# A new first list for a one-core attention and mixture kernel: loads of the seventh pair of token tiles placed earlier, GpSimd products for the sign words of eight weight chunks, TensorE low parts for the first eight chunks

## The chip, the cores and the metric

One core of one Trainium2 chip runs the kernel. The metric is device microseconds of one execution, as the median of several runs. In the profile PE is TensorE, DVE is VectorE, ACT is ScalarE, POOL is GpSimd and SP is SyncE, whose queue issues most of the transfers.

## The reference

Three stages follow one another. The first is attention inside chunks of 64 positions, the second a channel mixing layer, the third four experts of causal attention with a choice of two. The change lies in the part that does the first two. Batch is 8, sequence 576, eight heads of 64, 512 channels, 1024 hidden channels.

```python
scores = scale * np.matmul(q_c, k_c.transpose(0, 1, 2, 4, 3))   # 64 x 64 blocks
attn = softmax(scores)                                           # with max and 1e-9
out = np.matmul(attn, v_c)
...
xk = mu_k * x + (1.0 - mu_k) * x_prev
xr = mu_r * x + (1.0 - mu_r) * x_prev
k = np.maximum(xk @ w_k, 0.0)
v = k * k @ w_v
r = 1.0 / (1.0 + np.exp(-(xr @ w_r)))
x2 = r * v
...
out = _moe2_ref(x=x2, w_gate, wq, wk, wv, wo)
```

The weights w_r, w_k and w_v come as 64-bit floats. Each product of the mixing layer is formed from a high and a low fp32r part of both operands, three matmuls in place of one.

## The kernel before

The 4608 tokens are cut in 36 tiles of 128 for the attention and in 12 units of 384 for the mixing. Two tiles make a pair j. A pair's steps are, in the letters of the order lists: lq, lk, lv (loads through SP's queue, two buffers for each of q, k, v), Tq and Tk (transposes: by PE for tiles 0 to 11, by DVE for tiles 12 and later, since `by_dve` holds from the seventh pair on), Eq and Ek (ACT's copies out of PSUM), S (scores on PE), X, U, E, Z, Y (maximum, subtraction, exponential, sum, scaling), Tp and Ep (transposed probabilities), V (products with v on PE) and W (ACT's copies into the unit's tile XT). A unit's steps are prev (the column before a segment), a, b, c, d with r or k (ACT's scaled previous column, DVE's multiply-add, ACT's high part, DVE's low part of the mixed input, four channel groups each), r, k and v (12 matmuls each on PE; a k or an r needs all four d of its unit; v comes in two halves), s, K, J, y, z, x, D behind them.

The 20 weight chunks (128 x 512 numbers of 64 bits, 512 KB each) are turned into high and low parts on the way: chunks 0 to 3 belong to w_r, 4 to 11 to w_k, 12 to 19 to w_v. L loads a chunk, A (ACT) scales the upper words, G (DVE, two instructions, lines 430 and 431) puts sign and last bits together, B (DVE, line 435) joins, H (POOL, line 84) casts the high part, O (DVE, line 446) subtracts to get the low part. There are two buffers for the joined chunk (`cz`); O is the last to read one.

The order is written out. `follow(START)` emits the steps of the first list one by one, and `in_line` binds each instruction behind the one before it on its own engine, so that every engine and SP's queue run in the list's order, whatever waits. START covers the attention of tiles 0 to 11, units 0 and 1 and the beginning of unit 2, and all chunks; `TWO_UNITS` follows four times. Its first steps are Tq1 and Tq0, which there mean tiles 13 and 12. A step that waits holds up all behind it on its engine: a load that waits for a buffer holds up all later loads.

Of the kernel before, what the change touches and what calls it, by code (L numbers as in the profile page):

```python
# [20 lines left out]
START = """
L7 A7 G7 B7 L3 G3 L5 H7 O7 A3 B3 H3 lk0 L6 lq0 Tq0 L1 A5 G5 B5 L14 H5 lk1 Tk0 O3 A6 G6 B6 lq1 Eq0 L2 Tk1 H6 O5 G1 O6
A1 B1 A14 Ek1 G14 H1 O1 lk2 B14 H14 Ek0 G2 O14 Tq1 Eq1 S0 mu A2 B2 X0 H2 O2 lk3 L4 A4 Tk2 Ek2 U0 E0 G4 Z0 lq2 Tq2 lq3
Eq2 Tk3 lv1 B4 Y0 Tq3 L11 G11 H4 Ek3 Eq3 S1 X1 A11 B11 H11 Tp1 Ep1 U1 lv0 Tp0 O11 Ep0 lq5 Tq5 lq4 V0 O4 E1 Z1 Y1 W0 L0
Tq4 A0 lk5 G0 lk4 Tk5 L8 G8 Ek5 B0 Eq5 Eq4 H0 Tk4 Ek4 Tp3 Ep3 Tp2 Ep2 S2 X2 lv2 O0 lv3 L19 A8 V1 W1 prev0 U2 A19 G19
ar0,2 br0,2 ar0,0 br0,0 E2 Z2 cr0,2 dr0,2 lq7 Tq7 lk6 Tk6 Eq7 cr0,0 dr0,0 Y2 lq6 Tq6 Eq6 lk7 Tk7 Ek6 ar0,1 br0,1 ar0,3
Ek7 br0,3 cr0,1 lq8 Tq8 Tp4 B8 Ep4 lk8 S3 cr0,3 H8 Eq8 dr0,1 ak0,2 Tk8 Ek8 Tp5 lq9 Tq9 dr0,3 r0,0 r0,1 X3 bk0,2 lv5
ak0,1 Ep5 bk0,1 Eq9 U3 O8 ck0,2 ck0,1 lk9 Tk9 B19 H19 lv4 V2 dk0,1 dk0,2 E3 Z3 lq11 Tq11 s0,1 r0,2 r0,3 Ek9 S4 ak0,0
bk0,0 ak0,3 bk0,3 W2 prev1 ck0,3 ck0,0 L10 s0,3 G10 dk0,3 A10 s0,2 lk10 s0,0 dk0,0 k0,0 k0,1 k0,2 O19 L9 G9 B10 H10
ar1,0 lv7 br1,0 A9 B9 lk11 Tk11 lq10 Tq10 H9 Eq11 O10 L17 Y3 K0,0 O9 K0,1 J0,1 L18 cr1,0 dr1,0 A17 ar1,1 lk13 K0,2 G17  # L30
J0,0 ar1,2 A18 k0,3 Tp6 Ep6 br1,1 G18 k0,4 J0,2 lv6 k0,5 B18 H18 Tp7 cr1,1 K0,4 dr1,1 B17 O18 H17 J0,4 ar1,3 K0,3
br1,2 cr1,2 br1,3 k0,6 k0,7 cr1,3 K0,6 L13 A13 L12 O17 J0,3 K0,7 dr1,2 dr1,3 r1,0 r1,1 G13 A12 Ep7 B13 H13 Eq10 s1,0
L15 G12 B12 Ek11 V3 O13 J0,7 G15 s1,1 H12 O12 A15 W3 B15 L16 r1,2 Tk10 r1,3 A16 G16 Ek10 S5 s1,2 H15 O15 K0,5 B16 H16
lv9 ak1,1 J0,6 J0,5 s1,3 v0,0,0 O16 v0,0,1 ak1,3 bk1,3 X4 v0,1,0 v0,1,1 ck1,3 v0,2,0 v0,2,1 bk1,1 ck1,1 dk1,1 U4 ak1,0
E4 bk1,0 y0,1 z0,1 x0,1 D0,1 y0,0 dk1,3 ak1,2 bk1,2 ck1,0 dk1,0 v0,3,0 ck1,2 dk1,2 v0,3,1 k1,0 K1,0 z0,0 x0,0 y0,2
z0,2 D0,0 k1,1 K1,1 Z4 Y4 Tp9 Tp8 Ep8 y0,3 lv8 X5 J1,1 U5 k1,2 k1,3 x0,2 Ep9 K1,2 k1,4 k1,5 J1,2 D0,2 J1,0 K1,3 J1,3
K1,4 z0,3 x0,3 k1,6 k1,7 E5 J1,4 K1,5 K1,6 J1,5 K1,7 v1,0,0 J1,6 V4 W4 J1,7 v1,0,1 prev2 v1,1,0 ak2,1 D0,3 lv11 v1,1,1
v1,2,0 v1,2,1 Z5 Y5 Tp10 bk2,1 y1,0 ar2,2 br2,2 v1,3,0 cr2,2 v1,3,1 z1,0 y1,1 x1,0 D1,0 dr2,2 ar2,0 br2,0 ck2,1 dk2,1
cr2,0 dr2,0 ar2,3 br2,3 ar2,1 br2,1 Ep10 cr2,3 z1,1 x1,1 D1,1 Tp11 dr2,3 y1,2 z1,2 cr2,1 dr2,1 r2,0 r2,1 x1,2 ak2,3
bk2,3 ck2,3 dk2,3 s2,0 ak2,2 y1,3 ak2,0 s2,1 r2,2 r2,3 z1,3 lv10 Ep11 V5 s2,2 x1,3 D1,3 bk2,0 ck2,0 s2,3 bk2,2 ck2,2  # L40
lv13 lk12 D1,2 W5 lq13 lv12 lq12 dk2,0 dk2,2
""".split()
# [1001 lines left out]
```

## Time and profile before

| what | us |
|---|---|
| median of 3 runs | 1001.09 (1000.03 to 1002.81) |
| the profiled execution | 1000.0 |
| its span, first to last instruction | 998.0 |
| PE busy in the span | 946.5 (95%) |
| DVE, ACT, POOL busy | 670.2, 624.0, 192.2 |

PE is the bound of the whole, so what counts is where it waits or runs at the lower clock. The page's 40 slices show PE below nine tenths only in the first two slices and in slices 7 and 8 (150 to 200 us), apart from the last one; the granted clock falls below nine tenths of full speed in slices 2 and 8 alone. Nearly all else is a row of matmuls without a gap.

### The profile page before, as it was taken

The page shows a single profiled execution, that of the slowest core. Times are in us where ns is not written, and L with a number is a line of the kernel's source. Part 1 is how long each engine was busy: PE and PEld are TensorE (multiplying, and loading weights), DVE is VectorE, ACT ScalarE, POOL GpSimd, SP SyncE. Part 2 cuts the span into 40 slices and gives each one's busy share as a digit, 9 for nine tenths or more (in the row PEclk, how much of TensorE's full clock was granted, in tenths as well). Part 3 has the DMA queues.
Part 4 walks back from the last instruction along what each step waited for, and adds up shares of the span by engine and source line. Part 5 has one row for each costly group of instructions (what it writes and reads, how often), then busy time and mean ns, then how long its engine had stood idle before and what let it go on. Part 6 is the DMA issues. An engine that isn't in the chain of part 4 may idle for free.

```text
span 998.0 us, 21524 instructions
## 1 busy us (share of the span) xinstructions
PE 946.5 (95%) x8022; PEld 908.4 (91%) x8022; DVE 670.2 (67%) x1705; ACT 624.0 (63%) x1417; POOL 192.2 (19%) x336
## 2 busy tenths in 40 slices
PE   2699998699999999999999999999999999999997
PEld 2589998699999999999999999989989998998996
DVE  7899552565665557464747622688786787778885
ACT  3588364547675675657466924476675667567675
POOL 3112111020201111020202024323321233222101
PEclk9699999799999999999999999999999999999999
DMA  9875123453344334433413225565453645354312
GB/s 255 201 193 145 44 69 85 67 109 71 96 77 93 81 86 86 85 92 74 107 30 85 49 69 138 117 171 135 112 156 94 179 87 174 87 170 137 100 44 97
DMA packets 223408, 108.38 MB, mean 109 GB/s; under 512 B 187352, under 2 KB 199752, under 8 KB 223304
## 3 DMA queue, kind: packets, MB, share of 16 engines
q1 hardware_dynamic: 193032, 67.16, 29.7%
q0 software_dynamic: 30272, 39.86, 14.7%
...
## 4 chain that ended last, share of the span: by engine, by line
PE 84%; DVE 8%; DMA 3%; SPq 1%; ACT 1%; issue 1%; POOL 0%; ACTq 0%; POOLq 0%; DVEq 0%
PE mps L95 17%; PE mps L97 16%; PE mps L96 16%; PE pj L95 6%; PE pj L96 6%; PE pj L97 6%; PE Sps L747 4%; PE Tps L807 3%; PE AVps L840 2%; PE Tps L187 2%; PE AVps L836 2%; DMA st<-in_moe_w_k_dram 2%; PE PVps L267 1%; PE Sps L211 1%; DVE PTl L814 1%
## 5 line engine op out<-in xcount | busy, mean ns | idle before, releaser
L95 PE MATMUL mps<-xhk,wkh 128*128 128x384 f32 x384 | 131.9, 343 | 11.9 <-ACT r L364 11.9
L96 PE MATMUL mps<-xlk,wkh 128*128 128x384 f32 x384 | 129.9, 338 | 0.0
L97 PE MATMUL mps<-xhk,wkl 128*128 128x384 f32 x384 | 129.8, 338 | 0.0
L95 PE MATMUL mps<-kh,wvh 128*128 128x384 f32 x384 | 129.3, 338 | 0.0
L97 PE MATMUL mps<-kh,wvl 128*128 128x384 f32 x384 | 128.4, 334 | 0.0
L96 PE MATMUL mps<-kl,wvh 128*128 128x384 f32 x384 | 128.3, 334 | 0.0
L370 DVE TENSOR_TENSOR kl<-r,kh 128x384 fp32r<-128x384 f32 x96 | 54.0, 564 | 100.0 <-ACT kh L366 100.0
L759 ACT ACTIVATE P<-sm,nm 128x512 f32<-128x512 f32 (+3 forms) x144 | 83.7, 583 | 22.2 <-DVE nm L749 13.4
L84 POOL CAST x2d<-x2o 128x384 fp32r<-128x384 f32 x48 | 31.3, 653 | 316.1 <-DVE x2o L387 314.0
L749 DVE CUSTOM_DVE_ANT_0 sm<-Sps,mask 128x256 f32<-128x256 f32 (+4 forms) x160 | 74.8, 478 | 21.6 <-PE Sps L747 20.7
L95 PEld LDWEIGHTS mps<-xhk,wkh 128*128 128x128 f32 x384 | 73.0, 190 | 12.9 <-ACT r L364 12.5
L814 DVE TENSOR_TENSOR PTl<-Tps,PTh 128x512 fp32r<-128x512 f32 (+2 forms) x144 | 70.3, 506 | 5.8 <-ACT PTh L813 4.4
L96 PEld LDWEIGHTS mps<-xlk,wkh 128*128 128x128 f32 x384 | 73.0, 190 | 0.0
L97 PEld LDWEIGHTS mps<-xhk,wkl 128*128 128x128 f32 x384 | 72.9, 190 | 0.0
L95 PEld LDWEIGHTS mps<-kh,wvh 128*128 128x128 f32 x384 | 72.0, 188 | 0.7
L96 PEld LDWEIGHTS mps<-kl,wvh 128*128 128x128 f32 x384 | 72.1, 188 | 0.0
L97 PEld LDWEIGHTS mps<-kh,wvl 128*128 128x128 f32 x384 | 72.1, 188 | 0.0
L304 ACT ACTIVATE xa<-XT,mu 128x384 f32<-128x384 f32 x96 | 57.0, 615 | 23.4 <-DVE xlk L319 12.3
L308 DVE SCALAR_TENSOR_TENSOR xa<-XT,mu,xa 128x384 f32<-128x384 f32 x96 | 57.6, 621 | 18.4 <-ACT xa L304 18.1
L364 ACT ACTIVATE r<-mps 128x384 f32<-128x384 f32 x96 | 46.6, 485 | 34.5 <-PE mps L97 34.1
L813 ACT ACTIVATE PTh<-Tps 128x512 fp32r<-128x512 f32 (+2 forms) x144 | 61.7, 454 | 8.5 <-PE Tps L807 6.8
L95 PE MATMUL mps<-xhr,wrh 128*128 128x384 f32 x192 | 66.3, 345 | 0.0
...
## 6 DMA issues: line engine op xcount, KB each, us to landing
...
ldk<-in_k_dram SPq DMA_DIRECT2D x192, 32.0 KB
ldq<-in_q_dram SPq DMA_DIRECT2D x192, 32.0 KB
...
```

The source lines that it names most:

```text
L95: nc.tensor.matmul(out=out, lhsT=ah, rhs=bh, start=first and i == 0, stop=False)
L96: nc.tensor.matmul(out=out, lhsT=ah, rhs=bl, start=False, stop=False)
L97: nc.tensor.matmul(out=out, lhsT=al, rhs=bh, start=False, stop=last and i == n - 1)
L304: nc.scalar.activation(out=a, in_=XT[u][:, g, :, :SEG], func=ACTF.Copy, scale=mu1[:, w, g:g + 1])
L308: nc.vector.scalar_tensor_tensor(a, XT[u][:, g, :, 1:], mu[:, w, g:g + 1], a, op0=ALU.mult, op1=ALU.add)
L364: nc.scalar.activation(out=r, in_=MB.pop(("k", u, m)), func=ACTF.Relu)
L370: eng(nc, CFG["klo"][u >= CFG["nearly"]]).tensor_tensor(o.lo, K2.pop((u, m)), f32(o.hi), op=ALU.subtract)
L747: issued = nc.tensor.matmul(out=pp[:, :w], lhsT=x, rhs=y[:, a:a + w], start=n == 0, stop=n == len(terms) - 1)
L749: nc.vector.tensor_tensor_reduce(out=sm[:, a:a + w], in0=pp[:, :w], in1=mk[:, :w], op0=ALU.add, op1=ALU.min, scale=-scale, scalar=3e38, ac ...
L759: nc.scalar.activation(out=x[:, :nk], in_=sm[:, :nk], func=ACTF.Exp, scale=-1.0, bias=nm[:, :1], accum_out=z)
L813: nc.scalar.activation(out=h, in_=src, func=ACTF.Copy)
L814: nc.vector.tensor_tensor(l, src, f32(h), op=ALU.subtract)
```

## The change

Four things change. The first list is a new one: q and k of tiles 0 and 1 are loaded ahead of any chunk, chunks come in the order 3 14 2 8 0 7 1 5 10 11 6 4 18 9 16 13 12 19 15 17 (before: 7 3 5 6 1 14 2 4 11 0 8 19 10 9 17 18 13 12 15 16), and the loads of tiles 12 and 13 stand further forward. For the chunks 4, 6, 8, ..., 18 a new step M has POOL multiply the upper words, seen as f32, by zero in place, which leaves the sign bit alone; G is then one DVE instruction instead of two. For chunks 0 to 7 the low part is formed on PE by a new step PO: the joined chunk times the identity (plain f32) minus the high part times the identity (fp32r), summed in a PSUM bank of the three that r, k and v use; O is then ACT's copy out of that bank. A tile `minus`, minus the identity, is made once by ACT.

```diff
 START = """
-L7 A7 G7 B7 L3 G3 L5 H7 O7 A3 B3 H3 lk0 L6 lq0 Tq0 L1 A5 G5 B5 L14 H5 lk1 Tk0 O3 A6 G6 B6 lq1 Eq0 L2 Tk1 H6 O5 G1 O6
...
-lv13 lk12 D1,2 W5 lq13 lv12 lq12 dk2,0 dk2,2
+lq0 Tq0 lk0 Tk0 Ek0 lq1 lk1 Tq1 L3 Eq1 Tk1 Eq0 Ek1 S0 A3 G3 B3 H3 PO3 X0 U0 L14 A14 M14 G14 B14 H14 E0 Z0 O14 lk3 lq3
...
+LOW_BY_PE = (0, 1, 2, 3, 4, 5, 6, 7)
+SIGN_BY_POOL = (4, 6, 8, 10, 12, 14, 16, 18)
...
+        def c_sign(i):
+            h = f32(ST[i][0])
+            nc.gpsimd.tensor_scalar(h, h, 0.0, None, op0=ALU.mult)
+
         def c_bits(i):
             h, l = ST[i]
+            if i in SIGN_BY_POOL:
+                nc.vector.scalar_tensor_tensor(l, l, 29, h, op0=ALU.logical_shift_right, op1=ALU.bitwise_or)
+                return
             nc.vector.tensor_scalar(l, l, 29, None, op0=ALU.logical_shift_right)
             nc.vector.scalar_tensor_tensor(l, h, -(1 << 31), l, op0=ALU.bitwise_and, op1=ALU.bitwise_or)
...
+        minus = wkr.tile([128, 128], F32R, name="minus")
+        nc.scalar.activation(out=minus, in_=ident, func=ACTF.Copy, scale=-1.0)
+        LB = {}
+
+        def c_diff(i):
+            p = LB[i] = ps.tile([128, n], F32, tag="mix", bufs=3, name="lps")
+            nc.tensor.matmul(out=p, lhsT=ident, rhs=CZ.pop(i), start=True, stop=False)
+            nc.tensor.matmul(out=p, lhsT=minus, rhs=c_part(i)[0], start=False, stop=True)
+
         def c_lo(i):
             hi, lo = c_part(i)
+            if i in LOW_BY_PE:
+                nc.scalar.activation(out=lo, in_=LB.pop(i), func=ACTF.Copy)
+                return
             nc.vector.tensor_tensor(lo, CZ.pop(i), f32(hi), op=ALU.subtract)
...
-            L=c_load, A=c_scale, G=c_bits, B=c_join, H=c_hi, O=c_lo,
+            L=c_load, A=c_scale, G=c_bits, B=c_join, H=c_hi, O=c_lo, M=c_sign, PO=c_diff,
```

The changed kernel's lines are numbered two higher at first, 21 higher at the end. On SP's queue, at the end of the first list, the loads of 32 x 8 x 32 blocks are q and k of the tiles from 12 on (eight for a tile), those of v with 64 x 4 x 64 belong to tiles up to 11, those with 64 x 8 x 64 and 128 x 8 x 64 to tiles 13 and 12. Before:

```order
L566 DMA wst<-in_moe_wq_dram 128x4x64 x2
L174 DMA ldv<-in_v_dram 64x4x64 x8
L166 DMA ldv<-in_v_dram 64x8x64 x2
L151 DMA ldk<-in_k_dram 32x8x32 x8
L151 DMA ldq<-in_q_dram 32x8x32 x8
L166 DMA ldv<-in_v_dram 128x8x64
L151 DMA ldq<-in_q_dram 32x8x32 x16
```

After, at the same place:

```order
L153 DMA ldq<-in_q_dram 32x8x32 x8
L176 DMA ldv<-in_v_dram 64x4x64 x8
L153 DMA ldk<-in_k_dram 32x8x32 x8
L587 DMA wst<-in_moe_wq_dram 128x4x64 x2
L176 DMA ldv<-in_v_dram 64x4x64 x4
L153 DMA ldk<-in_k_dram 32x8x32 x8
L176 DMA ldv<-in_v_dram 64x4x64 x4
L153 DMA ldq<-in_q_dram 32x8x32 x8
L168 DMA ldv<-in_v_dram 64x8x64 x2
L168 DMA ldv<-in_v_dram 128x8x64
```

Before, three of the four loads of q and k for tiles 12 and 13 stood behind v of tile 13; now all four stand ahead of it, the last of them behind v of tile 11.

On DVE, the first rows of the program before (430, 431 are G, 435 is B, 446 is O):

```order
L430 TENSOR_SCALAR st<-st 128x512
L431 SCALAR_TENSOR_TENSOR st<-st 128x512
L435 SCALAR_TENSOR_TENSOR cz<-cz,st 128x512
L430 TENSOR_SCALAR st<-st 128x512
L431 SCALAR_TENSOR_TENSOR st<-st 128x512
L446 TENSOR_TENSOR wkl<-cz,wkh 128x512
L435 SCALAR_TENSOR_TENSOR cz<-cz,st 128x512
```

After (439, 440 are G's two, 437 is G's one, 444 is B, 467 is O where it is still DVE's, 226 and 232 are X and U):

```order
L439 TENSOR_SCALAR st<-st 128x512
L440 SCALAR_TENSOR_TENSOR st<-st 128x512
L444 SCALAR_TENSOR_TENSOR cz<-cz,st 128x512
L226 TENSOR_REDUCE m<-Sps 128x8 x2
L232 TENSOR_TENSOR P<-Sps,m 128x8x64 x2
L437 SCALAR_TENSOR_TENSOR st<-st 128x512
L444 SCALAR_TENSOR_TENSOR cz<-cz,st 128x512
L244 TENSOR_REDUCE m<-P 128x16
```

The first pair's softmax now comes after one chunk instead of after six, and no low part stands among the first rows.

On PE, from the first row on, after the change (216 is S, 272 is V, 459 and 460 are the two matmuls of PO):

```order
L189 MATMUL Tps<-ident,ldq 128x128 x4
L189 MATMUL Tps<-ident,ldk 128x128 x4
L189 MATMUL Tps<-ident,ldq 128x128 x4
L189 MATMUL Tps<-ident,ldk 128x128 x4
L216 MATMUL Sps<-kT,qT 64x64 x32
L459 MATMUL lps<-cz,ident 128x512
L460 MATMUL lps<-wrh,minus 128x512
L189 MATMUL Tps<-ident,ldq 128x128 x4
L189 MATMUL Tps<-ident,ldk 128x128 x4
```

Six of the eight PO stand ahead of the first matmul of r and two behind r's fourth step; ahead of that first matmul stand 24 groups of four transposes (before 25), four S and two V (as before).

## Rows read from the trace of the kernel before

**Rows 1.** PE's waits, whole run: who for whom, us in total, times, longest.

```profile
PE Tps L187 <- POOL wkh L84: 13.0, 1, 13.0
...
PE mps L95 <- ACT r L364: 11.9, 2, 11.3
```

**Rows 2.** Stretches: us, busy of PE, PEld, DVE, ACT, POOL, PEclk, DMA, GB/s.

```profile
0.00:57.60 57.60, 30.38 (x483) 25.28 (x484) 47.52 (x78) 30.25 (x55) 12.45 (x22) 0.82 0.91 220
57.60:162.70 105.10, 104.46 (x959) 102.08 (x957) 75.27 (x131) 70.21 (x138) 19.54 (x30) 1.00 0.39 106
171.20:182.50 11.30, 0.11 (x1) 0.00 (x0) 4.04 (x8) 0.89 (x2) 0.00 (x0) 0.61 0.51 86
182.50:187.20 4.70, 4.64 (x14) 4.64 (x15) 2.69 (x6) 4.51 (x11) 0.00 (x0) 0.50 0.43 67
187.20:191.80 4.60, 4.60 (x27) 4.60 (x27) 2.25 (x4) 4.15 (x9) 0.00 (x0) 0.97 0.42 66
```

**Rows 3.** Timeline of SP's queue, 160 to 200 us: start, us, instruction.

```profile
162.38 1.27 SPq L166 DMA_DIRECT2D ldv<-in_v_dram  x2
163.71 5.00 SPq L151 DMA_DIRECT2D ldk<-in_k_dram  x8
```

**Rows 4.** Timeline of DVE, 172 to 184 us; in brackets idle time before, releaser.

```profile
174.65 0.71 DVE L197 STREAM_TRANSPOSE qT<-ldq 128x512 f32<-128x512 f32 x1 [11.42 <-DMA ldq<-in_q_dram]
179.18 0.71 DVE L197 STREAM_TRANSPOSE qT<-ldq 128x512 f32<-128x512 f32 x1 [3.82 <-DMA ldq<-in_q_dram]
```

**Rows 5.** Timeline of PE, 181 to 192 us.

```profile
182.56 0.69 PE L95 MATMUL mps<-xhk,wkh 128*128 128x384 f32 x1 [11.26 <-ACT r L364]
```

**Rows 6.** Timeline, single rows of DVE and PE between 0 and 100 us.

```profile
5.11 0.43 DVE L430 TENSOR_SCALAR st<-st 128x512 int32<-128x512 int32 x1 [5.11 <-DMA st<-in_moe_w_k_dram]
...
57.65 0.42 PE L95 MATMUL mps<-xhr,wrh 128*128 128x384 f32 x1
...
99.16 0.45 PE L95 MATMUL mps<-kh,wvh 128*128 128x384 f32 x1
...
99.17 0.68 DVE L446 TENSOR_TENSOR wvl<-cz,wvh 128x512 fp32r<-128x512 f32 x1
```

**Rows 7.** Groups of instructions, shapes apart, 0 to 160 us: busy us, mean ns.

```profile
L431 DVE SCALAR_TENSOR_TENSOR st<-st 128x512 int32<-128x512 int32 x20 | 15.6, 779 | 0.7
L435 DVE SCALAR_TENSOR_TENSOR cz<-cz,st 128x512 int32<-128x512 int32 x20 | 14.5, 724 | 0.5
L308 DVE SCALAR_TENSOR_TENSOR xa<-XT,mu,xa 128x384 f32<-128x384 f32 x24 | 14.4, 620 | 3.4 <-ACT xa L304 3.2
...
L430 DVE TENSOR_SCALAR st<-st 128x512 int32<-128x512 int32 x20 | 9.3, 464 | 9.2 <-DMA st<-in_moe_w_k_dram 8.8 <-DMA st<-in_moe_w_v_dram 0.4
L84 POOL CAST wkh<-cz 128x512 fp32r<-128x512 f32 x8 | 7.7, 968 | 35.4 <-DVE cz L435 35.4
L446 DVE TENSOR_TENSOR wvl<-cz,wvh 128x512 fp32r<-128x512 f32 x8 | 5.4, 681 | 0.0
L453 POOL TENSOR_SCALAR mu<-mu 128x8 f32<-128x8 f32 x1 | 0.6, 616 | 0.0
```

**Rows 8.** The same groups on POOL, whole run.

```profile
L856 POOL TENSOR_TENSOR Yf<-Yf,zb 128x576 f32<-128x576 f32 x14 | 20.0, 1427 | 87.5 <-DVE Yf L851 79.9 <-DMA zb<-sc 4.7 <-DVE z L777 2.8
```

**Rows 9.** Line 431: durations in ns (shortest, median, longest); then timeline, 5 to 10 us.

```profile
L431 DVE SCALAR_TENSOR_TENSOR st<-st x20: 692/694/982, 5.6 to 95.7; 128x512 int32<-128x512 int32 x20
...
7.13 0.74 POOL L84 CAST wkh<-cz 128x512 fp32r<-128x512 f32 x1 [3.75 <-DVE cz L435]
...
7.44 0.98 DVE L431 SCALAR_TENSOR_TENSOR st<-st 128x512 int32<-128x512 int32 x1
```

**Rows 10.** The chain that ended last, in order of time: start, us, what.

```profile
136.62 1.09 PE PVps L270 x64
193.37 1.09 PE Sps L211 x64
259.79 0.87 PE Tps L187 x8
```

More of the change, by code (lines that the diff above doesn't have):

```diff
@@ L21 @@
 START = """
-L7 A7 G7 B7 L3 G3 L5 H7 O7 A3 B3 H3 lk0 L6 lq0 Tq0 L1 A5 G5 B5 L14 H5 lk1 Tk0 O3 A6 G6 B6 lq1 Eq0 L2 Tk1 H6 O5 G1 O6
[L23 to L40, printed above, removed]
-lv13 lk12 D1,2 W5 lq13 lv12 lq12 dk2,0 dk2,2
+lq0 Tq0 lk0 Tk0 Ek0 lq1 lk1 Tq1 L3 Eq1 Tk1 Eq0 Ek1 S0 A3 G3 B3 H3 PO3 X0 U0 L14 A14 M14 G14 B14 H14 E0 Z0 O14 lk3 lq3
@@ new lines @@
+Tq3 Eq3 O3 lq2 Y0 lk2 Tk3 Ek3 Tq2 Eq2 L2 G2 Tk2 Ek2 S1 X1 L8 A8 A2 B2 U1 M8 G8 B8 H2 Tp0 Ep0 lq5 Tp1 Ep1 lk5 Tk5 Tq5
+H8 lv1 lv0 Ek5 E1 Z1 Y1 Eq5 PO2 O2 V0 W0 lq4 Tq4 L0 Tp3 A0 Eq4 G0 B0 lk4 Tk4 Ek4 O8 L7 A7 Tp2 S2 G7 B7 X2 U2 Ep2 Ep3
+L1 G1 lv3 H0 PO0 O0 E2 A1 Z2 lv2 V1 W1 lq6 Tq6 Eq6 H7 PO7 mu prev0 ar0,3 B1 H1 PO1 ak0,0 Y2 br0,3 L5 L10 A5 cr0,3 lk7
+bk0,0 ck0,0 A10 Tk7 Ek7 lq7 M10 G5 Tp5 dk0,0 ar0,1 Ep5 B5 H5 dr0,3 ar0,0 br0,1 cr0,1 G10 Tq7 Eq7 lk6 Tk6 Ek6 br0,0
+cr0,0 dr0,1 ar0,2 O7 B10 O1 PO5 dr0,0 br0,2 cr0,2 S3 lk9 ak0,2 L11 A11 G11 Tp4 Tk9 Ek9 dr0,2 X3 O5 lq8 Tq8 Eq8 B11 lv4
@@ new lines @@
+L6 r0,0 r0,1 r0,2 H10 O10 ak0,3 A6 Ep4 U3 E3 lv5 V2 bk0,2 ck0,2 s0,1 bk0,3 H11 O11 M6 L4 A4 M4 G6 dk0,2 lk8 Tk8 ak0,1
+r0,3 lq9 s0,0 Tq9 s0,2 Z3 B6 lk11 Tk11 H6 Ek8 bk0,1 PO6 ck0,1 Eq9 ck0,3 G4 W2 B4 S4 L18 O6 Y3 A18 H4 PO4 O4 Tp6 Ep6
+Tp7 dk0,3 dk0,1 k0,0 k0,1 L9 X4 prev1 ar1,3 A9 ar1,2 K0,0 G9 k0,2 M18 G18 br1,3 B9 lq10 Tq10 br1,2 s0,3 B18 H18 J0,0
+cr1,3 cr1,2 K0,1 dr1,3 lk10 O18 k0,3 H9 O9 k0,4 U4 J0,1 dr1,2 lq11 Tq11 L16 A16 ar1,0 br1,0 M16 G16 K0,2 L13 G13 B16
+H16 lv6 K0,3 J0,3 A13 B13 H13 ar1,1 J0,2 Ep7 cr1,0 k0,5 k0,6 K0,5 k0,7 br1,1 cr1,1 lv7 K0,4 O16 J0,5 L12 A12 M12 dr1,0
@@ new lines @@
+O13 dr1,1 L19 G19 V3 A19 B19 Eq10 G12 B12 r1,0 K0,6 s1,0 H19 J0,6 O19 Tk10 L15 K0,7 H12 A15 O12 Ek10 L17 G15 B15 Eq11
+G17 lq12 r1,1 r1,2 r1,3 H15 O15 Ek11 S5 A17 s1,3 B17 J0,7 J0,4 H17 s1,1 O17 v0,0,0 v0,0,1 X5 U5 s1,2 v0,1,0 v0,1,1
+v0,2,0 E4 ak1,1 y0,0 ak1,2 bk1,2 ck1,2 dk1,2 v0,2,1 bk1,1 ak1,0 bk1,0 ck1,1 dk1,1 v0,3,0 ck1,0 y0,1 ak1,3 bk1,3 v0,3,1
+lv8 ck1,3 dk1,0 z0,1 dk1,3 k1,0 z0,0 x0,0 D0,0 x0,1 Z4 Y4 y0,2 E5 k1,1 z0,2 K1,0 J1,0 k1,2 x0,2 D0,2 Tp8 K1,1 Z5 Y5
+k1,3 K1,2 Ep8 J1,2 y0,3 z0,3 K1,3 J1,3 Tp9 D0,1 x0,3 k1,4 k1,5 K1,4 D0,3 k1,6 k1,7 J1,1 J1,4 Ep9 lv9 V4 K1,5 J1,5 lk12
@@ L42 @@
+K1,6 J1,6 v1,0,0 lv10 K1,7 J1,7 v1,0,1 v1,1,0 Tp10 v1,1,1 v1,2,0 v1,2,1 W3 lk13 y1,0 W4 prev2 ar2,3 br2,3 ar2,1 br2,1
+cr2,3 dr2,3 cr2,1 dr2,1 Ep10 z1,0 ar2,2 br2,2 y1,1 z1,1 v1,3,0 ak2,0 bk2,0 ck2,0 dk2,0 ar2,0 cr2,2 dr2,2 Tp11 v1,3,1
+x1,0 D1,0 br2,0 cr2,0 dr2,0 ak2,2 bk2,2 lv11 x1,1 D1,1 Ep11 r2,0 y1,2 ak2,3 bk2,3 s2,0 ck2,2 r2,1 s2,1 V5 y1,3 z1,3
+r2,2 r2,3 dk2,2 lq13 ak2,1 W5 bk2,1 ck2,1 ck2,3 lv13 z1,2 x1,3 x1,2 D1,2 s2,2 D1,3 lv12 dk2,1 dk2,3 s2,3
 """.split()
```

## The prediction

> **What bounds the kernel now.** I read the table of stretches first, to see where PE is not full. Up to 57.6 us, where the first matmul of r begins, PE is busy for 30.4 us at a mean granted clock of 0.82, while DVE is busy for 47.5 us and DMA is at 0.91; the following 105.1 us, to the end of what the first list gives PE, are full (104.5 us busy); then comes one hole of 11.3 us, and behind it 4.7 us at the lower level of the clock [rows 2]. The waits say the same: the 13.0 us at the very start and one wait of 11.3 us are the long ones [rows 1]. From 187 us on PE is close to full, so this change, which ends with the first list, can act in two places only: on when the first matmul of r begins, and on the hole.
>
> The hole is a queue's. SP issues v of tile 13 at 162.38 us, when the V just ahead of it on PE has given a buffer back, and only then the eight-part loads behind it [rows 3]. DVE, which transposes tiles 13 and 12 first of all in the next list, stands until 174.65 us for the one and until 179.18 us for the other, 11.42 and 3.82 us [rows 4]; behind them stands the multiply-add that ACT waits for, ACT frees a PSUM bank, and PE goes on at 182.56 us after 11.26 us [rows 5]. It goes on slowly: the first 4.64 us hold 14 matmuls, 0.33 us each, at a granted clock of 0.50 (1.2 GHz); the next 4.60 us hold 27, 0.17 us each, at 0.97, so nearly all at 2.4 GHz [rows 2]. 14 x 0.16 = 2.3 us go there. The place is worth 11.3 + 2.3 = 13.6 us.
>
> **The loads.** In the new order all four loads of q and k for tiles 12 and 13 stand ahead of v of tile 13. The last, q of tile 13, stands behind v of tiles 10 and 11 and k of tile 13, and these wait for the V at 136.62 us [rows 10]. Eight issues take 5.0 us [rows 3], the 24 from there on 15 us, so q of tile 13 is out by 153 us and is needed at 162.7. What is late next there is nothing that I can name: the d steps of unit 2 stand behind two r steps of PE work, as later lists have it, and those run without a hole. The cost of the added queueing is nothing, as SP is idle at that time but for waits. Gain: 13.6 us.
>
> **The start.** Here the vector engine sets the end, and I count its work ahead of r's first matmul. The first G instruction goes from 12 to 7, its second from 12 to 10 (three are the new single form), B from 11 to 9, O from 10 to 2, while one b and one d come to it; the three softmaxes stay. With 0.464, 0.779, 0.724, 0.681 and 0.620 us (d taken as b) [rows 7] that is -2.3 - 1.6 - 1.4 - 5.4 + 1.2 = -9.5 us. Of this six low parts moved to PE make 4.1 and three sign products moved to POOL 1.4; the rest is work put off until later.
>
> Against that the first chunk comes behind four q and k tiles, 4 x 256 KB; at the 220 GB/s of this stretch [rows 2] 4.8 us, so DVE starts at 9.9 instead of 5.11 us [rows 6]. With the same idle time of DVE as before the first matmul of r comes at 57.65 [rows 6] - 9.5 + 4.8 = 52.9 us.
>
> Two things come on top. The POOL product isn't in the trace. Its duration lies between the 0.62 us of the one small POOL scalar operation [rows 7] and the 1.43 us of an operation with two inputs on 576 numbers [rows 8]; the cast of the same 512 numbers takes 0.97 [rows 7], and I take 1.0. What it costs DVE I take from line 431, whose instructions last 0.69 us and at most 0.98; the one at 7.44 us lasts 0.98 and starts while a cast runs [rows 9]. That is 0.3 us each, three of them ahead of r, 0.9 us. And PE gets six PO. The fp32r matmul is 512/384 x 0.170 = 0.23 us [rows 2]. The plain f32 one is bounded below by the same 0.23 and above by the S step, where 32 plain products on 64 columns take 1.09 us [rows 10]: if four of them run side by side on quarters of the array, one takes 0.136 us, and eight times 64 columns 1.09 us. I take the upper end, the same data type, so PO is 1.3 us, or 2.6 at the lower clock. Six of them in a PE that is idle for 27 of 57.6 us would be free, were PE not bound to its order; at the lower clock PE has 30 + 16 = 46 us of work and can't start before the first tile lands near 6 us, so it comes to r at 52 us even without waits. PE is nearly as late as DVE, and I add 0.7 us. Together r begins at 54.5 us, between 51 (DVE's 5 us of idle time gets 3 us shorter) and 58 (PE waits as often as before): a gain of 3.1 us, between 6.6 and -0.4.
>
> **Between r and the second half of v.** PE gets two PO and one group of four transposes more: 2.6 + 0.4 (half of the 0.87 for eight [rows 10]) = 3.0 us lost, and 1.3 if PO takes its lower bound. DVE gets 3 fewer first and 2 more second G instructions, 2 more B, one b and one d less and one more pair's U (2 x 0.68, taken as O): -1.4 + 1.6 + 1.4 - 1.2 + 1.4 = +1.8 us. Before, DVE began the last low part that v's second half needs at 99.17 us, done at 99.85, and that half began 12 x 0.17 us [rows 2] after 99.16, at 101.2 [rows 6]: 1.4 us to spare, now 1.4 + 3.0 - 1.8 = 2.6. Five more products at 0.3 us take 1.5 of it. So no hole is forecast, but the margin is thin, and every PO also waits on PE's queue for POOL's cast; I set 1.0 us for that, between 0 and 4. The ACT copies that replace O go to an engine that was busy for 70 of 105 us [rows 2], and cost nothing unless a join waits for them.
>
> **Sum.** 1000.0 (the profiled execution; its span of 998.0 and 2.0 around it) - 13.6 - 3.1 + 3.0 + 1.0 = 987.3. The median of the three runs is 1.1 above the profiled one, so 988.4 in the runs' terms, told as 988.
>
> **Rivals.**
> First, the POOL product holds up DVE for all of its duration, not 0.3 us. The three ahead of r then cost 3.0 in place of 0.9, and five behind it 5.0 against 2.6 of margin, a hole of 2.4: 987.3 + 2.1 + 2.4 = 991.8, 993 in the runs' terms, and with 1.43 us and a spell at the lower clock 999. Against it: the long instruction at 7.44 us started 0.43 us before the cast from 7.13 to 7.87 us was over and ended at 8.42 us, 0.55 us later, which is less than the 0.69 it needs alone, so it didn't wait for all of the cast [rows 9]. The Trainium skill's page "SBUF — State Buffer", section "Who interferes with whom", gives the rule: a VectorE instruction with two SBUF inputs and a GpSimd instruction that reads SBUF take the shared pair in turn, for the whole instruction. By it moving the sign to POOL gains nothing, as a product of 1.0 us can hold DVE for longer than the 0.46 us saved.
>
> Second, another input of unit 2 is late where q of tile 13 was, say by 5 us with 2.3 us of lower clock behind it: 994.6, 996. For it: an order that is written out has no slack that mends itself. Against: later lists have no such hole.
>
> Third, the change doesn't do what it says: q of tile 13, behind two loads of v, is as late as before. Then the 13.6 us are not gained: 1000.9, 1002. Against it stand the 26 us between the V it waits for and the need.
>
> Fourth, slower: the POOL product is a slow operation. If it takes m us and DVE stands for all of it, the sum is -13.6 + (53.6 + 3m - 57.6) + 3.0 + (5m - 2.6) + 2.3 + 1.0, so 8m - 13.9 against before: nothing gained at 1.7 us, slower by more than 3 us from 2.1 us on; at 2.5 us 1006, 1007 in the runs' terms. For it: 0.62 us for 8 numbers [rows 7] shows a large fixed part. Against: two inputs and 576 numbers take 1.43 [rows 8].
>
> **Chances.** The forecast 0.70, with its own range of 983 to 994 (r between 51 and 58, holes of 0 to 4 us, PO at either bound, not all at once); the first rival 0.12 (990 to 999), the second 0.08 (996), the third 0.04 (1002), the fourth 0.06 (1007). A measurement tells 0.3% apart, 3.0 us here: faster means below 998.1. The forecast and the first two give 0.90 faster, the third 0.04 the same, the fourth 0.06 slower. The range of 983 to 997 leaves out the last two, a corner of the first rival and a tail on either side, some 2 in 10.
>
> **What would show it.** No wait of PE over 2 us between 150 and 200 us, and a granted clock of 1.0 there: the loads. The first matmul of r at 51 to 58 us; DVE's first chunk near 10 us; PO's plain matmul near 1.1 us at the higher level. PE full from r on, with no hole near the second half of v. POOL's product at 0.6 to 1.4 us, and two-input DVE instructions beside it 0.3 us longer. The prediction is wrong if r begins after 60 us, if a hole stands before v's second half, or if the DVE transposes of tiles 13 and 12 still wait for loads.

## The result, and the profile after

| | before | after |
|---|---|---|
| median of the runs, us | 1001.16 (1000.03 to 1002.81, 4 runs) | 985.9 (984.83 to 987.21, 4 runs) |
| profiled span, us | 998.0 | 983.9 |
| first matmul of r, us | 57.65 | 56.35 |
| first matmul of v, us | 99.16 | 100.83 |
| S of tiles 12 and 13 in unit 2, us | 193.30 | 180.29 |

The ratio is 0.9847, with a 95% interval of 0.9829 to 0.9865: 15 us faster, at 985.9 for a forecast of 988.0 in a range of 983 to 997.

First the table of stretches of after (us of each engine busy, with counts, then the granted clock, the share of the DMA engines and GB/s), cut at the first matmul of r and at the stretch where the hole stood:

```profile
core 0: us, PE busy (x) PEld busy (x) DVE busy (x) ACT busy (x) POOL busy (x), PEclk, DMA share, GB/s
0.00:56.30 56.30, 35.72 (x497) 25.65 (x498) 38.24 (x62) 32.56 (x61) 14.63 (x23) 0.91 0.86 204
56.30:162.70 106.40, 106.14 (x965) 102.79 (x964) 79.16 (x133) 73.34 (x142) 30.58 (x38) 1.00 0.48 120
171.20:191.80 20.60, 20.60 (x177) 20.28 (x177) 13.33 (x24) 14.44 (x26) 2.05 (x3) 1.00 0.44 77
```

From 171.2 to 191.8 us PE is full at a clock of 1.00, where before it stood for 11.3 us and ran 4.64 us at 0.50 behind that [rows 2]. Ahead of r DVE has 38.2 us of work in place of 47.5, yet r comes only 1.3 us earlier: DVE now idles for 18 us there, before for 10.

The waits of PE in the first 200 us (engine, line, tile, who released it: us in all, times, the longest) have no line of a few us behind the start; all but some 0.3 us of it lies ahead of r:

```profile
PE Tps L189 <- DMA ldq<-in_q_dram: 9.4, 5, 4.2
PE Tps L189 <- DMA ldk<-in_k_dram: 7.6, 4, 3.6
PE Sps L216 <- ACT kT L194: 2.2, 2, 1.2
PE PVps L272 <- ACT wrl L465: 0.4, 1, 0.4
PE lps L459 <- DVE cz L444: 0.3, 1, 0.3
```

And the place of the hole itself, from the order of time of SP's queue and of DVE: v of tiles 13 and 12 is still issued late, but nothing is queued behind it that DVE needs, and DVE's two transposes of tiles 13 and 12 (of q, and below of k) run back to back with no wait noted behind them, 13 us ahead of where they stood [rows 4]:

```profile
158.96 1.95 SPq L168 DMA_DIRECT2D ldv<-in_v_dram  x3
162.66 5.30 SPq L153 DMA_DIRECT2D ldq<-in_q_dram  x8
...
161.93 1.30 DVE L199 STREAM_TRANSPOSE qT<-ldq 128x512 f32<-128x512 f32 x2
163.15 1.26 DVE L199 STREAM_TRANSPOSE kT<-ldk 128x512 f32<-128x512 f32 x2
```

Between the two profiles the 14.1 us of span split by the marks in the first table: r starts 1.30 us earlier; from r to v PE takes 2.97 us more (44.48 for 41.51); from v to S of tiles 12 and 13 it takes 14.68 less (79.46 for 94.14); from there to the end 1.09 less (803.61 for 804.70).

### The profile page after: what moved, and what is told of

Read it like the earlier page. It is cut to its first block, busy times and chain, and to the rows that moved or that the text cites. A ratio compares the mean times of both kernels' runs of the same rounds, so it can differ in the third digit from the quotient of the medians.

```text
span 983.9 us, 21587 instructions
## 1 busy us (share of the span) xinstructions
PE 951.4 (97%) x8046; PEld 907.8 (92%) x8046; DVE 662.8 (67%) x1689; ACT 629.3 (64%) x1426; POOL 205.2 (21%) x344
## 4 chain that ended last, share of the span: by engine, by line
PE 87%; DVE 6%; DMA 4%; ACT 1%; issue 1%; SPq 0%; POOL 0%; ACTq 0%; DVEq 0%; POOLq 0%
PE mps L97 17%; PE mps L99 17%; PE mps L98 17%; PE pj L97 6%; PE pj L98 6%; PE pj L99 6%; PE Sps L768 4%; PE Tps L828 3%; DMA ldk<-in_k_dram 3%; PE Tps L189 2%; PE AVps L861 2%; PE AVps L857 2%; PE PVps L269 1%; PE Sps L213 1%; DVE PTl L835 1%; DVE sm L770 1%
## 5 line engine op out<-in xcount | busy, mean ns | idle before, releaser
L780 ACT ACTIVATE P<-sm,nm 128x512 f32<-128x512 f32 (+3 forms) x144 | 83.8, 583 | 21.5 <-DVE nm L770 13.2
L366 ACT ACTIVATE r<-mps 128x384 f32<-128x384 f32 x96 | 46.8, 487 | 35.7 <-PE mps L99 35.2
```

The source lines that it names most:

```text
L366: nc.scalar.activation(out=r, in_=MB.pop(("k", u, m)), func=ACTF.Relu)
L780: nc.scalar.activation(out=x[:, :nk], in_=sm[:, :nk], func=ACTF.Exp, scale=-1.0, bias=nm[:, :1], accum_out=z)
```

## The experiments

Each kernel differs from the one named in the list that sets the order (START), in one or both tables of chunks, or in a few lines. Of the lists only the places that differ are printed, without the names around them. The marks of all profiles stand together here (r and v: first matmul; DVE: busy us ahead of r, cut at the full tenth of a us; S: as above; "ahead of r": what PE waited for at the transposes of q that stand in the list just ahead of r). In the expectations of e5, e6, e8, e10, e11 and e12 the letters L and D mean: L, loads behind one another on SP's queue set the first matmul of r; D, the vector engine's work sets it. The other expectations say what their letters mean.

| run | median, us | ratio to before [95%] | r | DVE | v | S | ahead of r |
|---|---|---|---|---|---|---|---|
| before | 1001.16 | | 57.65 | 47.5 | 99.16 | 193.30 | no wait |
| after | 985.9 | 0.9847 [0.9829, 0.9865] | 56.35 | 38.2 | 100.83 | 180.29 | load of q, 1.59 |
| e1_loads_only | 987.76 | 0.9868 [0.9846, 0.989] | 60.72 | 48.7 | 102.23 | 182.63 | no wait |
| e2_parts_only | 1012.7 | 1.0115 [1.0098, 1.0132] | 68.50 | 42.6 | 111.82 | 207.27 | no wait |
| e3_list_only | 986.84 | 0.9863 [0.9842, 0.9885] | 56.69 | 42.4 | 101.55 | 181.36 | no wait |
| e4_loads_back | 995.9 | 0.9947 [0.9929, 0.9965] | 57.69 | 37.8 | 102.11 | 191.21 | load of q, 1.35 |
| e5_no_po | 986.06 | 0.9854 [0.9841, 0.9868] | 57.76 | 42.1 | 100.94 | 180.64 | no wait |
| e6_no_m | 984.52 | 0.9836 [0.982, 0.9851] | 55.64 | 38.6 | 100.62 | 180.46 | load of q, 1.89 |
| e7_po_six | 984.21 | 0.9831 [0.9813, 0.9848] | 54.46 | 38.1 | 98.53 | 178.22 | load of q, 1.23 |
| e8_v_by_pool | 987.54 | 0.9861 [0.9844, 0.9879] | 56.98 | 38.4 | 101.90 | 181.58 | load of q, 1.02 |
| e9_two_products | 987.5 | 0.9862 [0.9845, 0.9879] | 55.15 | 38.1 | 102.65 | 182.97 | load of q, 1.04 |
| e10_after_again | 985.32 | 0.984 [0.9825, 0.9855] | 56.58 | 38.2 | 101.58 | 181.04 | load of q, 1.60 |
| e11_v_early_by_pool | 983.2 | 0.9825 [0.9811, 0.9838] | 53.38 | 38.9 | 98.06 | 177.75 | load of q, 0.74 |
| e12_v_early_po_six | 981.36 | 0.9806 [0.9786, 0.9826] | 52.22 | 38.7 | 96.07 | 176.05 | load of q, 1.45 |

Lines of some of these kernels are numbered a few higher than in after, as their list is longer in lines. The runs were taken in groups on different chips, each beside the kernel before, whose median there was 1000.63 us (e1 to e4), 1001.55 (e7 to e10) and 1000.43 (e5, e6, e11, e12). Between groups the ratios are compared, not the times.

**The loads alone, and the loads put back.** e1 is the kernel before with three loads moved:

```
-bk2,2 ck2,2 lv13 lk12 D1,2 W5 lq13 lv12 lq12 dk2,0 dk2,2
+bk2,2 ck2,2 lk12 lq13 lq12 lv13 D1,2 W5 lv12 dk2,0 dk2,2
```

> The kernel before with one thing changed: k of tile 12 and q of tiles 13 and 12 are loaded ahead of v of tile 13 (and of nothing else); no POOL product, no PO, the old chunk order. Theory L (the gain is the hole of 11.3 us and the 2.3 us at the lower clock behind it, and the new first list with POOL's and TensorE's help is worth nothing on balance): span 984 to 985, within 1.5 us of the changed kernel's 983.9, no wait of PE over 2 us between 150 and 200 us, first matmul of r still at 57.6. Rival H (with the old list another input of unit 2 is late in the same place, so the loads alone give only a part): a hole of 3 to 8 us stays between 160 and 180 us, span 988 to 994.

987.76 us: the hole is gone, PE is full at a clock of 1.00 from 150 to 200 us, as the row of the table of stretches shows, where the kernel before had its 11.3 us of idle PE:

```profile
150.00:200.00 50.00, 50.00 (x406) 49.30 (x406) 33.98 (x63) 33.68 (x63) 7.26 (x12) 1.00 0.54 108
```

Its profile is 1.4 us longer than the 985 us expected at most, as r came at 60.72 us in it and not at 57.6; from v to S it takes 80.40 us in place of 94.14, 13.7 less. By the ratios 13.2 of the 15.3 us are in these three names, with an interval of 11.0 to 15.4, so nothing that can be told is left for the rest of the change. e4 does the reverse, the changed kernel with three loads back behind v, k of tile 13 staying ahead:

```
-lq12
-lk12
-lq13
...
-lv13 z1,2 x1,3 x1,2 D1,2 s2,2 D1,3 lv12 dk2,1 dk2,3 s2,3
+lv13 lk12 lq13 z1,2 x1,3 x1,2 D1,2 s2,2 D1,3 lv12 lq12 dk2,1 dk2,3 s2,3
```

> The changed kernel with the loads of q and k of tile 12 and q of tile 13 put back behind v of tile 13, everything else as changed. Theory L: the hole comes back in full, PE waits 9 to 12 us between 160 and 180 us and runs at the lower clock for some 5 us behind it: span 995 to 998, so about the kernel before. If the list and the parts carry a part of the gain by themselves, the span is below 993.

995.9 us, so by the ratios 10.0 of the 15.3 us go. The hole is back, with the same releaser, but at 7.5 us shorter than before and than the 9 to 12 us expected. That isn't SP's queue, which has the same loads in the same order behind v of tile 13 as before: the new list has the V that SP waits for ahead of two r steps of unit 2 and not behind them, 24 matmuls of 0.17 us, so PE has 13.9 us of work from that V on in place of 9.7. From the waits of PE and of DVE:

```profile
PE mps L106 <- ACT r L375: 7.5, 1, 7.5
...
DVE qT L208 <- DMA ldq<-in_q_dram: 13.4, 2, 9.6
```

S comes 10.9 us after that of the changed kernel: the 7.5 us of the hole, 1.3 from the start (57.69 for 56.35), and the rest, some 2, is the spell behind the hole, where the clock of 150 to 200 us is 0.93 in place of 1.00.

**The parts without the new list, and the list without the parts.** e2 has the old list with the new steps put into it, each M behind its A and each PO ahead of its O:

```
-H7 O7 A3
+H7 PO7 O7 A3
...
-O3 A6 G6
+O3 A6 M6 G6
```

In chunks 8 and 10 the product stands behind the instruction that uses it, so the low parts of these two chunks aren't the reference's; the instructions are the same.

> The changed kernel's code with the old first list: behind each A of chunks 4, 6, ..., 18 stands the POOL product, ahead of each O of chunks 0 to 7 stands PO; loads as before. Theory D (the vector engine's work sets the start): eight low parts (5.4 us) and three sign instructions (1.4 us) less ahead of r, so r begins near 51 us instead of 57.6; the hole stays, and the span is 998.0 - 6.8 = 991 to 993. Theory W (the start waits for loads and for PE's order, so work taken off DVE comes back as waits): r begins within 2 us of 57.6, span 996 to 1000.

1012.7 us, slower than the kernel before, which neither theory had. r comes 10.9 us later, at 68.50, and the hole of 11.2 us stays. The waits of PE and of DVE up to 260 us name the new steps: PE waits for the join that its plain product reads, DVE for POOL's product:

```profile
PE mps L106 <- ACT r L375: 11.9, 2, 11.2
PE lps L468 <- DVE cz L453: 10.4, 4, 7.4
...
DVE st L446 <- POOL st L441: 16.3, 6, 5.8
```

Work taken off DVE is no gain where the list then makes two in-order engines wait for each other. e3 is the opposite, the new list with its loads and without the names M and PO, three low parts moved to where DVE has room:

```
-LOW_BY_PE = (0, 1, 2, 3, 4, 5, 6, 7)
-SIGN_BY_POOL = (4, 6, 8, 10, 12, 14, 16, 18)
+LOW_BY_PE = ()
+SIGN_BY_POOL = ()
```

> The changed kernel with its new list, loads moved as there, but without the POOL products and without PO: all signs and low parts by DVE (the O of chunks 7, 1 and 5 stand a little further forward, ahead of the A that takes over their buffer). Theory D: 5.5 us more of DVE work ahead of r, so r at 60 to 62 us, and a hole ahead of v's second half as five signs and two low parts add 3.7 us there; PE saves two PO, 2.2 us: span 988 to 993. Theory W: DVE waits 16 us for loads ahead of r in the changed kernel and takes the 5.5 us out of that, r at 56 to 58 us; behind r the 3.7 us find only 0.5 us of margin, a hole of some 3 to 5 us: span 983 to 988.

986.84 us, within 1 us of after, with r at 56.69 as theory W had it: both offloads together are worth little. It is also within 1 us of e1, which has the old list with the loads moved, so what the new list is worth beyond its loads can't be told either. e5 takes away the low parts on PE alone, and e6 the products on POOL alone, each with its names in the list:

```
-LOW_BY_PE = (0, 1, 2, 3, 4, 5, 6, 7)
+LOW_BY_PE = ()
```

> The changed kernel with all eight low parts by the vector engine, in places of the list where nothing waits twice: 8 x 0.68 us more on the vector engine, six of them ahead of r, eight PO fewer on TensorE, two of them behind r. Theory D: r comes 4.1 us later, at 60.5 us, and behind r 2.2 us of TensorE's work go while the vector engine gets 1.4 us more: 987 to 989 us. Theory L: r within 1.5 us of 56.4, the time 985 to 986.5 us, so that TensorE's low parts are worth nothing on balance.

```
-SIGN_BY_POOL = (4, 6, 8, 10, 12, 14, 16, 18)
+SIGN_BY_POOL = ()
```

> The changed kernel with the sign of all chunks by the vector engine, no product on POOL: 8 x 0.46 us more on the vector engine, three of them ahead of r, 12.8 us less on POOL. Theory D: r 1.4 us later, and behind it 2.3 us more against a margin of 0.5 at the second half of v: 987.5 to 989 us. Theory L: r within 1 us of 56.4, the time 985 to 987 us. If POOL's products hold the vector engine for most of their 1.60 us, this run is the faster one by 2 us or more: under 983.5.

e5 takes 986.06 and e6 984.52 us; their ratios, 0.9854 and 0.9836, lie beside 0.9847 and 0.9840 for the changed kernel, and neither can be told from it. What differs is how r comes about. These are rows of PE ahead of r, in order of time (start, us; the idle time ahead and its releaser in brackets), first of after, then of e5:

```profile
52.20 1.16 PE L216 MATMUL Sps<-kT,qT 64*64 64x64 f32 x64 [0.96 <-ACT kT L194]
...
55.97 0.63 PE L189 MATMUL Tps<-ident,ldq 128*128 128x128 f32 x4 [1.59 <-DMA ldq<-in_q_dram]
56.35 0.44 PE L97 MATMUL mps<-xhr,wrh 128*128 128x384 f32 x1
```

```profile
53.38 1.98 PE L225 MATMUL Sps<-kT,qT 64*64 64x64 f32 x64 [2.48 <-ACT kT L203]
...
55.77 0.63 PE L198 MATMUL Tps<-ident,P 128*128 128x128 f32 x2
56.20 1.06 PE L198 MATMUL Tps<-ident,ldk 128*128 128x128 f32 x4
57.05 1.06 PE L198 MATMUL Tps<-ident,ldq 128*128 128x128 f32 x4
57.76 0.67 PE L106 MATMUL mps<-xhr,wrh 128*128 128x384 f32 x1
```

With PO, PE stands and waits for a load of q before it can go on to r. In after SP issued that load at 49.73 us, behind a weight chunk and two loads of k that had kept its queue from 42.31 to 48.77. Without PO, and in the kernel before, there is no such wait: PE comes to the loads late, from S and the transposes behind it, that is from ACT, DVE and its own work, and r comes 1.2 us later than in the nearest profile of the changed kernel. A part of that is the clock: from the start of S to r e5 takes 4.4 us without a wait, and after 2.6 beside its wait of 1.59, as these matmuls run at a granted clock of 0.50 in e5 (53.38 to 57.76 us) and of 1.00 in after (52.20 to 56.35), that is at the lower and at the higher of its two levels. So before it was in the main PE's and DVE's own work that set the start; with 9.3 us less of it on DVE a load comes last, and the loads are nearly as late. That the loads alone hold r there is argued from these waits and from e11 below, and not shown by itself.

**The start by the loads.** In after, SP needs 8.62 us to issue v of tiles 0 and 1, the weight chunk behind it is late, and DVE stands for it (SP's queue and DVE, in order of time):

```profile
16.21 8.62 SPq L176 DMA_DIRECT2D ldv<-in_v_dram  x8
24.94 1.27 SPq L160 DMA_DIRECT2D ldq<-in_q_dram  x2
26.26 0.62 SPq L422 DMA_DIRECT2D st<-in_moe_w_r_dram  x1
...
32.48 0.43 DVE L439 TENSOR_SCALAR st<-st 128x512 int32<-128x512 int32 x1 [4.52 <-DMA st<-in_moe_w_r_dram]
```

Of the 8.62 us the first issue alone takes 4.00, and each of the others 0.6 to 0.7. From 20 to 40 us the DMA engines are busy for 0.65 of the time. e8 has these eight issues on POOL's queue, at the same place in the list:

```
-                nc.sync.dma_start(out=x[p:p + n], in_=v[b, :, s:s + n, :].rearrange("h p d -> p h d"))
+                (nc.gpsimd if t < 2 else nc.sync).dma_start(out=x[p:p + n], in_=v[b, :, s:s + n, :].rearrange("h p d -> p h d"))
...
-                    nc.sync.dma_start(out=x[r * 64:(r + 1) * 64, c],
+                    (nc.gpsimd if t < 2 else nc.sync).dma_start(out=x[r * 64:(r + 1) * 64, c],
```

> The changed kernel with the loads of v of tiles 0 and 1 issued on POOL's queue, ahead of nothing that POOL has to wait for, in place of SP's, where those eight issues last 8.62 us and stand ahead of a weight chunk for which the vector engine then waits 4.5 us. Theory L (in the changed kernel the first matmul of r is set by loads, each behind the other on SP's queue, not by the vector engine's amount of work): what stands behind is issued some 8 us earlier, the vector engine's wait of 4.5 us is gone or under 1 us, r begins at 52 to 54 us instead of 56.35, and the time falls by 2 to 4 us, to 982 to 984 us. Theory D (the vector engine's work and the tensor engine's order set it, as the prediction's sum has it): the wait only moves, r begins at 55.5 us or later, the time is within 1 us of the changed kernel's 985.9.

987.54 us, and r at 56.98: r where D expected it, the time 0.6 us beyond D's bound, and for another reason. DVE's wait for the weight chunk is gone, but POOL, itself in order, came to the issues at 24.99 us only, so v is late. PE waits for v, ACT for PE, and DVE for ACT (PE's row, then DVE's two):

```profile
31.71 2.54 PE L272 MATMUL PVps<-PT,ldv 64*64 64x64 f32 x64 [5.42 <-DMA ldv<-in_v_dram]
...
27.94 0.44 DVE L439 TENSOR_SCALAR st<-st 128x512 int32<-128x512 int32 x1
...
35.85 0.69 DVE L444 SCALAR_TENSOR_TENSOR cz<-cz,st 128x512 int32<-128x512 int32 x1 [6.73 <-ACT cz L428]
```

e11 moves the two names ahead as well, to a place where POOL is idle:

```
-H8 lv1 lv0 Ek5
+H8 Ek5
...
-B14 H14 E0 Z0
+B14 H14 lv1 lv0 E0 Z0
```

> The changed kernel with v of tiles 0 and 1 issued on POOL's queue, and the two loads moved ahead to behind POOL's second cast, at some 16 us, where POOL stands idle for 4.4 us; in the earlier form of this POOL came to them at 25 us only and v itself was 5.4 us late. Theory L (loads in their row set the first matmul of r): v lies ready when the first V comes at 26 us, the weight chunk behind it is issued some 5 us earlier, the vector engine's wait of 4.5 us is gone and nothing takes its place: r at 52 to 54 us instead of 56.35 and 56.58, the time 982 to 983.5 us. Theory D (the vector engine's work and the tensor engine's order set it): r at 55.5 us or later, the time within 1 us of the changed kernel's 985.3 to 985.9.

983.2 us (982.33 to 983.96), and r at 53.38, 3.0 us earlier than in after, with DVE's work ahead of it no smaller (38.9 us). By the ratios, 0.9825 for 0.9847 and 0.9840, 1.5 to 2.2 us are gained; the intervals overlap, and the changed kernel itself was not run on this chip. The runs alone therefore don't settle it, and neither does one profile's r; but the two profiles with v early, this one and e12's, have r at 53.38 and 52.22, and the four with the same list up to r but for v between 54.46 and 57.69. POOL issues v from 15.97 us on, DVE takes the same chunk without a wait, and the next wait is 0.91 us (POOL, then DVE, in order of time):

```profile
15.97 5.07 POOL L185 DMA_DIRECT2D ldv<-in_v_dram  x8
...
29.13 0.42 DVE L448 TENSOR_SCALAR st<-st 128x512 int32<-128x512 int32 x1
29.59 0.72 DVE L449 SCALAR_TENSOR_TENSOR st<-st 128x512 int32<-128x512 int32 x1
31.22 0.69 DVE L453 SCALAR_TENSOR_TENSOR cz<-cz,st 128x512 int32<-128x512 int32 x1 [0.91 <-ACT cz L437]
```

That is what theory L expected: loads moved, DVE's work unchanged, r earlier by what the wait lost less some new small ones. The long issue isn't gone: here the first load of q behind takes 4.49 us on SP, so what went from SP are eight issues of some 0.6 us. PE still waits for a load of q just ahead of r, 0.74 us.

**TensorE's low parts behind r.** e7 is the changed kernel with two low parts back on DVE, those of chunks 4 and 6, the two that PE computes behind the first matmul of r:

```
-LOW_BY_PE = (0, 1, 2, 3, 4, 5, 6, 7)
+LOW_BY_PE = (0, 1, 2, 3, 5, 7)
```

> The changed kernel with the low parts of chunks 4 and 6, the two that TensorE computes behind the first matmul of r, by the vector engine again: 2 x 1.09 us less on TensorE, 2 x 0.68 us more on the vector engine. Theory W (TensorE is full from r on, so its work counts one for one and the vector engine still keeps ahead): 983.7 us, no wait before the second half of v. Theory M (the margin of 0.5 us at the second half of v is used up: v comes 2.2 us earlier, its last weight chunk 1.4 us later): a hole of about 3 us before the second half of v, 986 to 987 us.

984.21 us, 1.1 below the changed kernel beside it (985.32), so between the theories, and the runs of the two overlap (983.09 to 985.55 against 984.81 to 986.11). Its profile is 2.6 us shorter, but 2.1 of that came ahead of r (54.46 for 56.58), where its list is the same as the changed kernel's. From r to v it takes 44.07 us, against 44.48 and 45.00 in the two profiles of the changed kernel: of the 2.2 us taken off PE it keeps 0.4 to 0.9, and a new wait for DVE takes the largest part of the rest:

```profile
PE Tps L198 <- DVE P L259: 1.1, 1, 1.1
```

e12 has both, the edit of e11 and that of e7: v early on POOL's queue and six low parts on PE.

> The same with the low parts of chunks 4 and 6 by the vector engine again, as in the run with six low parts on TensorE, which took 984.2 us. If both act for themselves the time is 1.1 us below the run with v on POOL's queue alone: 981 to 982.5 by theory L, 984 to 984.5 by theory D. If v comes earlier and the vector engine then has no margin left at the second half of v, a wait of 1 to 3 us stands there and the time is that of the run with v alone.

981.36 us (978.49 to 983.79, 4 runs): faster than the kernel before by 1.9% (0.9806, 0.9786 to 0.9826), where theory L expected it if both act for themselves. Of the kernels that ran it has the lowest median. That it beats e11 isn't shown, as their runs overlap, and of the 2.3 us between their profiles 1.2 came ahead of r, where their lists are the same.

**POOL's product, twice.** e9 carries out each of POOL's eight products two times:

```
             nc.gpsimd.tensor_scalar(h, h, 0.0, None, op0=ALU.mult)
+            nc.gpsimd.tensor_scalar(h, h, 0.0, None, op0=ALU.mult)
```

> The changed kernel with each of POOL's eight products by zero carried out twice, one behind the other (the result is the same), so POOL works 12.8 us more. If a product costs the vector engine only what its rows show, some 0.3 to 0.5 us where a short one-input instruction starts beside it, the eight more cost 0 to 2 us where the vector engine has no slack: r begins within 1.5 us of 56.35, the time is 985 to 988. If the product holds the vector engine for all of its 1.60 us (the first rival), the three ahead of r cost 4.8 us more and the five behind it 8 us against a margin of 0.5 us at the second half of v: r at 61 us, a hole near 7 us at v, 996 or more.

987.5 us, 2.2 more than the changed kernel beside it (985.32, e10 below), and r no later (55.15). Sixteen products last 13.8 and 13.4 us in place of 12.8. Had each held DVE for its length, DVE's instructions would read several us longer; ahead of r they are 38.1 us for 38.2, and from r to v 42.2 for 42.1. What was lost lies between r and v, 47.50 us for 44.48 and 45.00, and there DVE waits for the second product, ahead of the instruction that reads it (DVE's waits of 56 to 104 us; the changed kernel has no such line there):

```profile
DVE st L438 <- POOL st L433: 3.5, 3, 1.5
```

That refutes the first rival, a product that holds DVE for all of its duration.

**The changed kernel once more**, beside e7, e8 and e9:

> The changed kernel itself once more, so that the others of this group stand beside it on the same chip: 985 to 987 us. Theory L expects the first matmul of r to stray by some 1 to 3 us from 56.35 us between profiles, with the loads, as it did between two profiles of one start (57.65 and 60.72 us, 56.35 and 57.69 us); theory D expects it within 0.5 us.

985.32 us, and r at 56.58, within 0.23 of the first profile, as theory D expected of it; but the two profiles of this one kernel differ less than those of kernels that share its start (54.46 in e7, 57.69 in e4).

## Why the prediction was right, point by point

**The hole, 13.6 us forecast.** Right in place and size. From v to S of tiles 12 and 13 the changed kernel takes 14.68 us less; 0.6 of it is a wait of PE for ACT between 104 and 125 us that the kernel before had and the changed one hasn't, and 14.1 is left for the hole with its slow spell. e1 shows that the three moved loads do this alone (13.7 us less, with the 0.6 us wait still there), e4 that most of it goes when they go back. Nothing else was late there, so the second rival and the third, that q of tile 13 stays late, are out.

**The start, 3.1 us forecast, 1.3 measured.** This is the term that was mis-sized. The first chunk at 9.9 us was right (9.76), and so was the work taken off DVE: 47.5 - 38.2 = 9.3 us, for 9.5 less 0.9 for POOL's products. The step that failed is "with the same idle time of DVE as before": DVE's idle time ahead of r grew by 8.0 us, from 10 to 18. Of that 4.7 are at the very start, as the sum had them; the other 3.4 on balance are not in the sum, and one wait alone, for a weight chunk behind v's eight issues on SP, lasts 4.52. The sum asked what DVE does, and not what is late next when DVE is quicker: the loads, as the 1.59 us ahead of r and e11 show. The 56.35 us lie in the range of 51 to 58, whose upper part stood for PE waiting as before. The 0.7 us for PE's order were spent on a thing that wasn't there: PE waited for loads and not for its own amount of work.

**Between r and v, 3.0 us forecast.** 2.97 measured, from nearly the right parts: a PO is shorter than taken. From the start of one to that of the next it takes 44.47 - 43.38 = 1.09 us at the higher level of the clock, which I had at 1.3 (PE's rows, in order of time):

```profile
43.38 1.02 PE L459 MATMUL lps<-cz,ident 128*128 128x512 f32 x2
43.84 0.80 PE L460 MATMUL lps<-wkh,minus 128*128 128x512 f32 x1
44.47 1.02 PE L459 MATMUL lps<-cz,ident 128*128 128x512 f32 x2
```

Two of them make 2.2 in place of 2.6, and with 0.4 for the transposes 2.6; the 0.4 left over is the PE idle of 106.40 - 106.14 = 0.26 us and the spread between profiles, which is as large (44.48 and 45.00 in the two of one kernel).

**The waits behind r, 1.0 us allowed.** No hole came at the second half of v, but little was left of the margin. The last low part that it needs ends at 102.27 + 0.68 = 102.95 us; v began at 100.83, and its second half begins 12 x 0.17 us later, at 102.9, with the chunk in question among its first products. I had 2.6 less 1.5, so 1.1 us; it was some half of one. The 1.0 us wasn't spent.

**POOL's product.** Its duration was outside my bounds, 1.604 us for 0.62 to 1.43; the nearest row was the one that moved more numbers, and the bound should have reached beyond it, since the operation was another. The fourth rival turned at 1.7 us if DVE stood for all of it, so its duration alone was close to deciding. It didn't, because DVE didn't stand. These are POOL's products and DVE's rows beside them:

```profile
L432 POOL TENSOR_SCALAR st<-st 128x512 f32<-128x512 f32 x8 | 12.8, 1604 | 15.3 <-ACT cz L428 15.3
...
47.87 1.78 POOL L432 TENSOR_SCALAR st<-st 128x512 f32<-128x512 f32 x1 [2.16 <-ACT cz L428]
...
48.28 0.98 DVE L444 SCALAR_TENSOR_TENSOR cz<-cz,st 128x512 int32<-128x512 int32 x1
...
79.77 1.60 POOL L432 TENSOR_SCALAR st<-st 128x512 f32<-128x512 f32 x1 [1.35 <-ACT cz L428]
...
80.68 0.54 DVE L372 TENSOR_TENSOR kl<-r,kh 128x384 fp32r<-128x384 f32 x1
...
90.04 1.60 POOL L432 TENSOR_SCALAR st<-st 128x512 f32<-128x512 f32 x1 [3.12 <-ACT cz L428]
...
90.07 0.92 DVE L439 TENSOR_SCALAR st<-st 128x512 int32<-128x512 int32 x1
91.03 0.69 DVE L440 SCALAR_TENSOR_TENSOR st<-st 128x512 int32<-128x512 int32 x1
```

The two-input join that starts 0.41 us behind a product's start lasts 0.98 us in place of 0.69, which is the 0.3 us that I took from the row beside a cast [rows 9]. The one-input instruction that starts 0.03 us behind one lasts 0.92 in place of 0.43. The two-input instructions that start 0.91 and 0.99 us into a product last 0.54 and 0.69 us, as they do alone. The same holds in the profiles of e7, e9, e10, e11 and e12: of the DVE instructions that stand in rows of their own, those that start in the first 0.46 us of a product last 0.08 to 0.49 us longer, with one input or two, and those that start 0.49 us into it or later don't. So a product costs 0 to 0.5 us, and when the DVE instruction starts decides, not how many inputs it has. The Trainium skill's rule that the two engines take a shared pair in turn for the whole instruction (page "SBUF — State Buffer", section "Who interferes with whom") isn't borne out here: DVE is held for a part of a product of 1.6 us, by these rows, and e9's doubled products add nothing to DVE's busy time.

**The end.** From S of tiles 12 and 13 on nothing was forecast, and 1.09 us were gained. That stretch takes 804.70 us in the profile of before and 802.6 to 803.8 in all the others. One of these is e2, with the old loads and the old list (802.8), and the changed kernel's own two profiles differ by 0.8 there (803.61 and 802.86). So it isn't shown that the change has a part in the 1 us; what it is stays open.

**The sum.** The profiled run of after took 985.7 us, 1.6 below the 987.3 of the sum: 1.0 for waits not spent, 1.1 at the end, 0.5 in the hole and 0.6 for the wait of ACT make 3.2, less 1.8 at the start, 1.4; the other 0.2 lies around the span, 1.8 us in place of 2.0. The 1.1 us that I added to get from the profiled run to the median weren't there: the median is 985.9.
